# Reordering the loads and splitting one stripe of layer 1 in a fused linear-attention and MLP kernel

## The chip, the cores and the metric

The kernel runs on one core of a Trainium2 chip. The metric is the device time of one execution in microseconds. The kernel before falls into two groups, about 263 us (262.9 to 264.0) and about 265.8 us (265.2 to 266.6). A trace is one execution; its span is about 1.7 us shorter than the time of that execution (263.5 of 265.2 us).

Names used below: TensorE is PE in the profile, its weight loads PEld; VectorE is DVE, ScalarE ACT, GpSimd POOL, and SP issues most transfers. SMELU is the smooth ReLU between the two layers; relu on ScalarE is its first part. A cast turns float32 into bf16.

## The reference

Lightning attention with a decay per head, then a two-layer MLP with a smooth ReLU:

```python
# q, k, v: (4, 8, 768, 64) float32, decay lam: (8,)
# attention, per block: (q kT * decay mask) v + (q * decay) state;  state = decay * state + kT v
x = attn_out.transpose(0, 2, 1, 3).reshape(3072, 512)
h = x @ w_in                      # 512 x 2048
g = where(h >= 1, h, where(h <= -1, 0, (h + 1) ** 2 / 4))
out = g @ w_out                   # 2048 x 512
```

## The kernel before

The 3072 tokens are 24 chunks of 128; four chunks make a stripe of 512 tokens. A chunk has two units `u` (four heads each), and a unit three stages. T transposes q (`pq`), computes kT and the state update in one matmul (`pk`), and copies them out of PSUM. S computes the scores (`ps`) from kT and masks them (`sc`). O computes the output (`po`) and copies it into `xT`, which layer 1 reads. In these traces TensorE ran its instructions in program order, ready or not: in the kernel before, the masked scores of chunk 3's last O were there at 29.5 us, but this O ran at 41.9 us, after chunk 4's `pk` at 41.5 us, which stands before it in the program.

```python
def load(c):                                   # 3 x 256 KB, runs of 256 B, on the SP queue
    for name, src in (("q", q), ("k", k), ("v", v)):
        t = ld.tile([128, H, D], F32, ...)     # 6 buffers each
        nc.sync.dma_start(out=t, in_=...)

def load_w_in(i):  nc.gpsimd.dma_start(...)    # 4 pieces, float32 -> bf16, POOL queue
def load_w_out(i): nc.gpsimd.dma_start(...)    # 4 pieces

def cast(c, k_eng):                            # qs on POOL, ks on DVE or POOL, v on ACT
    ...
    nc.scalar.copy(out=vi[c % NV][:, :, 0, :], in_=vf...)
# ... (cut: stage_t, stage_s, stage_o)
def l1(s, ni):      # four 128x512 matmuls into ph, relu on ACT; smelu: three DVE operations per pair
def l2(s, i):       # four 128x512 matmuls into py
# ...
    ensure_loaded(CPS - 1)                     # CPS = 4 chunks per stripe
    for c in range(CPS):
        ensure_cast(c, nc.vector)
        if c >= 1:
            load_w_in(state["wi"]); state["wi"] += 1
        for _ in range(4): ...                 # attention of chunk c, alone
    load_w_in(state["wi"])
    for i in range(WS): load_w_out(i)
    ensure_loaded(CPS + 1); ensure_cast(CPS)
    a, b_ = att_step()                         # T of chunk 4, then O of chunk 3
    ensure_loaded(CPS + PF)                    # PF = 5
    for s in range(NST + 1):
        for i in range(FO):                    # 16 steps a stripe
            # sub-steps due by now, two a unit: even T(u) and O(u-1), odd S(u); casts one chunk ahead
            if s < NST: l1(s, i)
            for f in todo_a: f()               # T or S
            if s < NST: smelu(s, i)
            if s > 0:   l2(s - 1, i)
            for f in todo_b: f()               # O
```

So in a full stripe each step holds four layer-1 matmuls of stripe s, four layer-2 matmuls of stripe s-1 and half an attention unit.

Of the kernel before, what the change touches and what calls it, by code (L numbers as in the profile page):

```python
# [9 lines left out]
BF16 = mybir.dt.bfloat16  # L10
I32 = mybir.dt.int32
AX = mybir.AluOpType
AF = mybir.ActivationFunctionType


def _bc(ap, idx, n):

    a = list(ap.ap)
    a = a[:idx] + [[0, n]] + a[idx:]
    return bass.AP(ap.tensor, ap.offset, a)  # L20
# [3 lines left out]
def kernel(  # L24
# [16 lines left out]
    nc = tc.nc  # L41
    B, H, S, D = q.shape
    C = 128
# [5 lines left out]
    KO = d_model // 128  # L49
    FO = d_ff // 128  # L50
    MS = 512
    NST = n_tok // MS
    NCH = n_tok // C
    CPS = MS // C
    NU = NCH * 2

    const = ctx.enter_context(tc.tile_pool(name="const", bufs=1))
    big = ctx.enter_context(tc.tile_pool(name="big", bufs=1))
    ld = ctx.enter_context(tc.tile_pool(name="ld", bufs=6))
    qkp = ctx.enter_context(tc.tile_pool(name="qkp", bufs=3))  # L60
    ktp = ctx.enter_context(tc.tile_pool(name="ktp", bufs=3))
    scp = ctx.enter_context(tc.tile_pool(name="scp", bufs=2))
# [14 lines left out]


    qkv_ld = {}

    def load(c):
        b, s0 = c // NCB, (c % NCB) * C
        ts = []
        for name, src in (("q", q), ("k", k), ("v", v)):
            t = ld.tile([128, H, D], F32, name=f"{name}f", tag=f"{name}f")
            nc.sync.dma_start(out=t, in_=src[b, :, s0:s0 + C, :].rearrange("h p d -> p h d"))
            ts.append(t)
        qkv_ld[c] = ts

    lam_b = const.tile([128, H], F32)  # L90
    nc.sync.dma_start(out=lam_b, in_=lam.partition_broadcast(128))
    load(0)
# [44 lines left out]

    def load_w_in(i):
        n = d_ff // WS
        nc.gpsimd.dma_start(out=w_in_sb[:, :, i * n:(i + 1) * n], in_=w_in_r[:, :, i * n:(i + 1) * n])  # L140

    def load_w_out(i):
        n = FO // WS
        nc.gpsimd.dma_start(out=w_out_sb[:, i * n:(i + 1) * n, :], in_=w_out_r[:, i * n:(i + 1) * n, :])


    qs, ks = {}, {}

    def cast(c, k_eng):
        qf, kf, vf = qkv_ld.pop(c)  # L150
        cb = c % NCB
        t = qkp.tile([128, H, D], BF16, name="qs", tag="qs")
        nc.gpsimd.tensor_tensor(t, qf, _bc(tab_q[:, cb, :], 2, D), op=AX.mult)  # L153
        qs[c] = t
        t = qkp.tile([128, H, D], BF16, name="ks", tag="ks")
        k_eng.tensor_tensor(t, kf, _bc(tab_k[:, cb, :], 2, D), op=AX.mult)  # L156
        ks[c] = t
        nc.scalar.copy(out=vi[c % NV][:, :, 0, :], in_=vf.rearrange("p (a b) d -> p a (b d)", b=2))  # L158

# [2 lines left out]
    def stage_t(u):  # L162
        c, hf = u // 2, u % 2
        cb = c % NCB
        pq = pp_q.tile([128, 2, 128], BF16, name="pq", tag="pq")
        pk = pp_k.tile([128, 2, 2, 128], F32, name="pk", tag="pk")
        for j in range(2):
            hp = 2 * hf + j
            nc.tensor.transpose(out=pq[:, j, :], in_=qs[c][:, 2 * hp:2 * hp + 2, :].rearrange("p a d -> p (a d)"),  # L169
                                identity=ident)  # L170
        for j in range(2):
            hp = 2 * hf + j
            nc.tensor.matmul(pk[:, j], lhsT=ks[c][:, 2 * hp:2 * hp + 2, :].rearrange("p a d -> p (a d)"),  # L173
                             rhs=vi[c % NV][:, hp], start=True, stop=True)
        qb = qbd[u % NQ]
        for hi in range(2):
            nc.scalar.copy(out=qb[hi * 64:hi * 64 + 64, :, hi, :], in_=pq[hi * 64:hi * 64 + 64])  # L177
        t = ktp.tile([128, 2, 128], BF16, name="kT", tag="kT")
        nc.scalar.copy(out=t, in_=pk[:, :, 1, :])  # L179
        kT[u] = t  # L180
        if cb < NCB - 1:
            t = up.tile([128, 2, 128], BF16, name="U", tag=f"U{hf}")
            if cb == 0:
                nc.vector.tensor_copy(t, pk[:, :, 0, :])
            else:
                nc.vector.tensor_tensor(t, pk[:, :, 0, :], U[u - 2], op=AX.add)  # L186
            U[u] = t
# [10 lines left out]
    def stage_o(u):  # L198
        c, hf = u // 2, u % 2
        cb = c % NCB  # L200
        st, off = c // CPS, (c % CPS) * C
        po = pp_o.tile([128, 2, 2, 128], F32, name="po", tag="po")
        for j in range(2):
            hp = 2 * hf + j
            if cb > 0:
                nc.tensor.matmul(po[:, j], lhsT=U[u - 2][:, j, :], rhs=qbd[u % NQ][:, j], start=True, stop=False)  # L206
            nc.tensor.matmul(po[:, j], lhsT=vi[c % NV][:, hp, 0, :], rhs=sc_sb[u][:, 2 * j:2 * j + 2, :],  # L207
                             start=(cb == 0), stop=True)
        if st not in xT:
            xT[st] = xp.tile([128, KO, MS], BF16, name="xT", tag="xT")  # L210
        for hi in range(2):
            nc.scalar.copy(out=xT[st][hi * 64:hi * 64 + 64, 2 * hf:2 * hf + 2, off:off + C],  # L212
                           in_=po[hi * 64:hi * 64 + 64, :, hi, :])

    def att(i):

        u, odd = i // 2, i % 2
        a, b_ = [], []
        if not odd:
            if u < NU:  # L220
                a.append(lambda: stage_t(u))
            if 1 <= u <= NU:
                b_.append(lambda: stage_o(u - 1))
        elif u < NU:
            a.append(lambda: stage_s(u))
        return a, b_


    gT, r_t, py_t = {}, {}, {}

    def l1(s, ni):
        ph = pp_h.tile([128, MS], F32, name="ph", tag="ph")
        for ko in range(KO):
            nc.tensor.matmul(ph, lhsT=w_in_sb[:, ko, ni * 128:(ni + 1) * 128], rhs=xT[s][:, ko, :],  # L234
                             start=(ko == 0), stop=(ko == KO - 1))
        if ni % 2 == 0:
            r_t[s] = rp.tile([128, 2, MS], BF16, name="r", tag="r")
        nc.scalar.activation(out=r_t[s][:, ni % 2, :], in_=ph, func=AF.Relu, bias=one[:, 0:1])  # L238

    def smelu(s, ni):  # L240
        if ni % 2 == 0:
            return
        r = r_t[s]
        if ni == 1:
            gT[s] = gp.tile([128, FO, MS], BF16, name="gT", tag="gT")
        t = rp.tile([128, 2, MS], BF16, name="t1", tag="t1")
        nc.vector.tensor_scalar(t, r, 0.5, 1.0, op0=AX.mult, op1=AX.min)
        w = rp.tile([128, 2, MS], BF16, name="w1", tag="w1")
        nc.vector.tensor_tensor(w, r, t, op=AX.subtract)  # L249
        nc.vector.tensor_tensor(gT[s][:, ni - 1:ni + 1, :], w, t, op=AX.mult)  # L250

    def l2(s, i):
        ms, kg = i // 4, i % 4
# [10 lines left out]
            nc.sync.dma_start(out=out[m0:m0 + 128, :], in_=o)  # L264


    PF = 5
    state = {"ld": 2, "cast": 0, "att": 0, "wi": 0, "wo": 0}

    def ensure_loaded(c):  # L270
        while state["ld"] <= min(c, NCH - 1):
            load(state["ld"])
            state["ld"] += 1

    def ensure_cast(c, k_eng=None):
        while state["cast"] <= min(c, NCH - 1):
            cast(state["cast"], k_eng or nc.gpsimd)
            state["cast"] += 1

    def att_step():  # L280
        a, b_ = att(state["att"])
        state["att"] += 1
        return a, b_

    NSUB = 2 * NU + 1


    ensure_loaded(CPS - 1)
    for c in range(CPS):
        ensure_cast(c, nc.vector)  # L290
        if c >= 1:
            load_w_in(state["wi"])
            state["wi"] += 1
        for _ in range(4):
            a, b_ = att_step()
            for f in a + b_:
                f()
    load_w_in(state["wi"])
    for i in range(WS):
        load_w_out(i)  # L300
    ensure_loaded(CPS + 1)
    ensure_cast(CPS)
    a, b_ = att_step()
    for f in a + b_:
        f()
    ensure_loaded(CPS + PF)

    def target(g):

        base = 4 * CPS + 1  # L310
        if g < 16:
            return base + (18 * (g + 1)) // 16
        return min(NSUB, base + 18 + (g - 15))

    for s in range(NST + 1):
        for i in range(FO):
            g = s * FO + i
            todo_a, todo_b = [], []
            while state["att"] < min(NSUB, target(g)):
                c = state["att"] // 4  # L320
                ensure_loaded(c + PF)
                ensure_cast(c + 1)
                a, b_ = att_step()
                todo_a += a
                todo_b += b_
            if s < NST:
                l1(s, i)
            for f in todo_a:
                f()
            if s < NST:  # L330
                smelu(s, i)
            if s > 0:
                l2(s - 1, i)
            for f in todo_b:
                f()


# [28 lines left out]
```

## Time and profile before

| | before |
|---|---|
| time, median of the comparison | 263.62 us (263.03 to 265.84) |
| span of the trace | 263.5 us (an execution of 265.2 us, near the slower group) |
| TensorE busy | 85% |
| first layer-1 matmul | 43.2 us |
| second, third, fourth, fifth stripe begin (first layer-1 matmul that runs beside layer 2, and each 16 steps on) | 78.0, 113.3, 148.6, 183.7 us |
| last layer-1 stripe begins | 217.9 us |

The page's slices cut the span into 40 parts of 6.6 us; a digit is the busy share in tenths. PEclk is the granted TensorE clock; before the first clock record of a trace (22.7 us here) the page counts it as full, which is no measurement.

```profile
PE   0567306666889999999999999999999999999993
...
ACT  4768303778996977797779777977796754554210
...
PEclk9999755999999999999999999999999999999998
DMA  6999999999990526753574357110111011111122
```

From the thirteenth slice on TensorE is full up to the end of the kernel. But for that end, all its idle time is in the first 78 us, in which the DMA engines are full (90% or more in the slices from 6.6 to 79 us). The waits of TensorE in that part, longest first (columns: who waited for whom, total us, times, longest us):

```profile
PE pk L173 <- ACT vi_152 L158: 12.6, 1, 12.6
PE pq L169 <- POOL qs L153: 6.7, 1, 6.7
PE ps L192 <- ACT kT L179: 5.0, 8, 1.9
```

The 12.6 us are chunk 4's v, which landed at 40.9 us behind the weights. Chunk 3's O stands behind chunk 4's T in TensorE's order, so layer 1 could not start either.

In the steady part nothing waits. This is one unit of attention there, on TensorE alone (start, duration, operation):

```profile
116.11 0.28 PE L169 MATMUL pq<-ident,qs 128*128 128x128 bf16 x2
116.22 0.38 PE L173 MATMUL pk<-vi_152,ks 128*128 128x256 bf16 x2
116.44 1.03 PE L258 MATMUL py<-w_out_sb,gT 128*128 128x512 bf16 x4
117.31 0.38 PE L207 MATMUL po<-sc,vi_150 128*128 128x256 bf16 x2
117.53 1.03 PE L234 MATMUL ph<-xT,w_in_sb 128*128 128x512 bf16 x4
118.39 0.38 PE L192 MATMUL ps<-qbd_148,kT 128*128 128x256 bf16 x2
```

The durations overlap: the four `py` matmuls from 116.44 us are listed with 1.03 us, and `po` starts 0.87 us after them. The pace is the difference of starts. Between the transposes (`pq`) and the scores (`ps`) of the unit lie 2.28 us, filled with a layer-2 group, an older O and a layer-1 group. In that time ScalarE copies q (0.74 us) and kT (0.37 us).

### The profile page before, as it was taken

The numbers are of one execution on the slowest core, as the hardware profiler recorded it, in microseconds if no ns is written. First come the engines' busy times: TensorE is split into PE (matmuls) and PEld (weight loads), VectorE is DVE, ScalarE is ACT, GpSimd is POOL, SyncE is SP. The second block draws the span as 40 slices with busy tenths as digits, with TensorE's granted clock in tenths as the row PEclk, the third lists the DMA queues.
The fourth block names the chain that finished last, engine by engine and source line by source line (L and its number), as shares of the span: only waits on it lengthen the run. The fifth ranks groups of instructions, "written<-read, shape, count | busy, mean of one in ns | idle before, by whom it ended". The sixth has DMA issues, their size and how long they took to land.

```text
span 263.5 us, 3576 instructions
## 1 busy us (share of the span) xinstructions
PE 222.8 (85%) x1209; PEld 118.7 (45%) x1232; DVE 143.8 (55%) x245; ACT 173.7 (66%) x389; POOL 54.2 (21%) x61
## 2 busy tenths in 40 slices
PE   0567306666889999999999999999999999999993
PEld 0234203333445555555555555555555544444441
DVE  3554201388887576657574766574747645555300
ACT  4768303778996977797779777977796754554210
POOL 3418111552340332033303320333000000000000
PEclk9999755999999999999999999999999999999998
DMA  6999999999990526753574357110111011111122
GB/s 134 210 217 187 196 196 220 210 226 218 218 202 2 138 67 120 159 128 85 108 159 121 88 113 163 40 40 0 42 41 40 2 40 40 40 42 40 40 80 80
DMA packets 82721, 29.58 MB, mean 112 GB/s; under 512 B 75536, under 2 KB 79632, under 8 KB 82704
## 3 DMA queue, kind: packets, MB, share of 16 engines
q1 hardware_dynamic: 78480, 25.18, 45.5%
q0 software_dynamic: 4224, 4.19, 9.7%
q8 instruction: 9, 0.15, 0.3%
q14 instruction: 8, 0.07, 0.1%
HBM read 27.27 MB, written 6.29 MB: 127 GB/s over the span
## 4 chain that ended last, share of the span: by engine, by line
PE 69%; DVE 3%; ACT 1%; issue 0%; ACTq 0%
PE py L258 31%; PE ph L234 26%; PE po L207 3%; PE ps L192 3%; PE pk L173 2%; PE po L206 2%; PE pq L169 1%; DVE gT L250 1%; DVE w_726 L249 1%; DVE sc L195 0%; DVE w_768 L249 0%; ACT r L238 0%; DVE U L186 0%; ACT xT L212 0%; ACT osb L262 0%
## 5 line engine op out<-in xcount | busy, mean ns | idle before, releaser
L234 PE MATMUL ph<-xT,w_in_sb 128*128 128x512 bf16 x380 | 99.6, 383 | 1.7 <-ACT r L238 1.3
L238 ACT ACTIVATE r<-ph,one 128x512 bf16<-128x512 f32 x96 | 65.9, 687 | 43.3 <-PE ph L234 39.6
L258 PE MATMUL py<-w_out_sb,gT 128*128 128x512 bf16 x365 | 92.3, 379 | 1.0
L234 PEld LDWEIGHTS <-w_in_sb 128*128 128x128 bf16 x384 | 37.9, 99 | 37.6 <-issue 2.8
L258 PEld LDWEIGHTS <-gT 128*128 128x128 bf16 x384 | 37.6, 98 | 32.3
L153 POOL TENSOR_TENSOR qs<-qf,tab_q 128x512 bf16<-128x512 f32 x24 | 25.3, 1052 | 121.7 <-PE pq L169 92.0
L186 DVE TENSOR_TENSOR U<-pk,U 128x256 bf16<-128x256 f32 x32 | 13.6, 424 | 56.5 <-ACT kT L179 56.5
L212 ACT CAST xT<-po 64x256 bf16<-64x256 f32 x96 | 35.3, 367 | 4.5 <-PE po L207 3.7
L195 DVE TENSOR_TENSOR sc<-ps,causal 128x512 bf16<-128x512 f32 x48 | 32.9, 685 | 4.6 <-PE ps L192 4.0
L156 POOL TENSOR_TENSOR ks<-kf,tab_k 128x512 bf16<-128x512 f32 x20 | 22.3, 1117 | 7.9 <-DMA kf<-in_k_dram 7.9
L262 ACT COPY osb<-py 128x512 f32<-128x512 f32 x24 | 14.2, 591 | 12.4 <-PE py L258 12.4
L169 PE MATMUL pq<-ident,qs 128*128 128x128 bf16 x96 | 14.3, 235 | 6.7 <-POOL qs L153 6.7
L179 ACT CAST kT<-pk 128x256 bf16<-128x256 f32 x48 | 17.9, 372 | 2.4 <-PE pk L173 1.3
L173 PE MATMUL pk<-vi_152,ks 128*128 128x256 bf16 x32 | 6.8, 298 | 14.6 <-ACT vi_152 L158 12.6
L169 PEld LDWEIGHTS <-qs 128*128 128x128 bf16 x96 | 10.1, 106 | 16.8 <-POOL qs L153 6.7
L173 PEld LDWEIGHTS <-ks 128*128 128x128 bf16 x96 | 8.1, 103 | 20.5 <-issue 8.1
L192 PEld LDWEIGHTS <-kT 128*128 128x128 bf16 x96 | 8.5, 101 | 19.4 <-ACT kT L179 11.0
L158 ACT CAST vi_152<-vf 128x512 bf16<-128x512 f32 x8 | 4.9, 610 | 11.9 <-DMA vf<-in_v_dram 11.9
L177 ACT COPY qbd_146<-pq 64x256 bf16<-64x256 bf16 x32 | 11.6, 361 | 1.6 <-PE pq L169 1.2
L177 ACT COPY qbd_144<-pq 64x256 bf16<-64x256 bf16 x32 | 11.5, 361 | 0.6 <-PE pq L169 0.2
L177 ACT COPY qbd_148<-pq 64x256 bf16<-64x256 bf16 x32 | 11.5, 361 | 0.5
L206 PEld LDWEIGHTS <-U 128*128 128x128 bf16 x80 | 8.2, 102 | 7.8 <-issue 3.7
(187 smaller groups left out, 213.9 us busy)
## 6 DMA issues: line engine op xcount, KB each, us to landing
qf<-in_q_dram SPq DMA_DIRECT2D x24, 256.0 KB, 4.8
kf<-in_k_dram SPq DMA_DIRECT2D x24, 256.0 KB, 4.7
vf<-in_v_dram SPq DMA_DIRECT2D x24, 256.0 KB, 5.0
out_dram<-osb SPq DMA_DIRECT2D x24, 256.0 KB, 2.0
w_in_sb<-in_moe_w_in_dram POOLq DMA_DIRECT2D x4, 512.0 KB, 8.7
w_out_sb<-in_moe_w_out_dram POOLq DMA_DIRECT2D x4, 512.0 KB, 15.5
lam_b<-in_lam_dram SPq DMA_DIRECT2D x1, 4.0 KB, 2.9
```

Source lines behind the costliest of these rows:

```text
L153: nc.gpsimd.tensor_tensor(t, qf, _bc(tab_q[:, cb, :], 2, D), op=AX.mult)
L156: k_eng.tensor_tensor(t, kf, _bc(tab_k[:, cb, :], 2, D), op=AX.mult)
L169: nc.tensor.transpose(out=pq[:, j, :], in_=qs[c][:, 2 * hp:2 * hp + 2, :].rearrange("p a d -> p (a d)"), identity=ident)
L173: nc.tensor.matmul(pk[:, j], lhsT=ks[c][:, 2 * hp:2 * hp + 2, :].rearrange("p a d -> p (a d)"), rhs=vi[c % NV][:, hp], start=True, stop=True)
L177: nc.scalar.copy(out=qb[hi * 64:hi * 64 + 64, :, hi, :], in_=pq[hi * 64:hi * 64 + 64])
L179: nc.scalar.copy(out=t, in_=pk[:, :, 1, :])
L192: nc.tensor.matmul(ps[:, 2 * j:2 * j + 2, :], lhsT=kT[u][:, j, :], rhs=qbd[u % NQ][:, j], start=True, stop=True)
L195: nc.vector.tensor_tensor(t, ps, _bc(causal, 1, 4), op=AX.mult)
L212: nc.scalar.copy(out=xT[st][hi * 64:hi * 64 + 64, 2 * hf:2 * hf + 2, off:off + C], in_=po[hi * 64:hi * 64 + 64, :, hi, :])
L234: nc.tensor.matmul(ph, lhsT=w_in_sb[:, ko, ni * 128:(ni + 1) * 128], rhs=xT[s][:, ko, :], start=(ko == 0), stop=(ko == KO - 1))
L238: nc.scalar.activation(out=r_t[s][:, ni % 2, :], in_=ph, func=AF.Relu, bias=one[:, 0:1])
L258: nc.tensor.matmul(py, lhsT=gT[s][:, ko, ms * 128:(ms + 1) * 128], rhs=w_out_sb[:, ko, :], start=(ko == 0), stop=(ko == FO - 1))
```

## The change

The intent is to load in the order of need: four token chunks, w_in, four chunks, w_out, the rest. Two loads of SP wait for a weight piece of the POOL queue. While w_out is not there, layer 1 runs alone, and for that stripe 1 is split into halves of 256 tokens, so that its first half needs only chunks 4 and 5. The core of the diff:

```diff
+            if after is not None:
+                tc.add_manual_dep(d.ins, after.ins.name, SYNC)
...
+    nc.scalar.preload_act_table_set("natural_log_exp_and_others")
...
+    items = []                      # t, s, o of every unit, in TensorE's order
+    for u in range(NU):
+        if u % 2 == 0 and u > 0:
+            items += [("o", u - 1), ("t", u)]
+        else:
+            items += [("t", u)] + ([("o", u - 1)] if u > 0 else [])
+        items.append(("s", u))
...
+    def att_to(n):
+        while st["it"] < min(n, len(items)):
+            kind, u = items[st["it"]]
+            if kind == "t" and u % 2 == 0:
+                cast_to(u // 2)                           # casts on demand
+            fns[kind](u)
+            if kind == "s" and u % 2 == 1 and st["ahead"]:
+                cast_to(u // 2 + 1)                       # a chunk ahead, later on
...
+        if c == 1:
+            load_w_in(0); load_w_in(1)
+        elif c == 2:
+            load_w_in(2); load_w_in(3)
+            load_to(CPS, after=w_dma[2])
+            load_to(2 * CPS - 1)
+
+    run(zip_(full(0)[:10], []), 0)                        # layer 1 alone
+    run(zip_(full(0)[10:], []), done(CPS) - st["it"])     # with chunk 4
+    att_to(done(CPS + 1))                                 # chunk 5 alone
+    run(zip_(half(1, 0), []), done(2 * CPS - 1) - st["it"])   # with chunks 6, 7
+    for i in range(WS):
+        load_w_out(i)
+    load_to(2 * CPS, after=w_dma[WS + 2])
+    load_to(2 * CPS + LD - 1)
+    st["ahead"] = True
+    run(zip_(half(1, 1), []), 0)                          # alone
+    run(zip_([], l2s(0)), done(3 * CPS - 1) - st["it"])   # layer 2 with chunks 8 to 11
+    for s in range(2, NST + 1):
+        a = done(min((s + 2) * CPS, NCH) - 1)
+        run(zip_(full(s) if s < NST else [], l2s(s - 1)), a - st["it"])
```

(`run` spreads the attention items over the half-steps; cuts are marked with dots.)

More of the change, by code (lines that the diff above doesn't have):

```diff
@@ L55 @@
     NU = NCH * 2
+    LD = 6
     const = ctx.enter_context(tc.tile_pool(name="const", bufs=1))
     big = ctx.enter_context(tc.tile_pool(name="big", bufs=1))
-    ld = ctx.enter_context(tc.tile_pool(name="ld", bufs=6))
+    ld = ctx.enter_context(tc.tile_pool(name="ld", bufs=LD))
     qkp = ctx.enter_context(tc.tile_pool(name="qkp", bufs=3))
@@ L79, with load @@
     qkv_ld = {}
-    def load(c):
+    w_dma = []
+    SYNC = mybir.DependencyInfo(mybir.DependencyClass.Sync, mybir.DependencyReason.DATA)
+    def load(c, after=None):
         b, s0 = c // NCB, (c % NCB) * C
@@ L85, in load @@
             t = ld.tile([128, H, D], F32, name=f"{name}f", tag=f"{name}f")
-            nc.sync.dma_start(out=t, in_=src[b, :, s0:s0 + C, :].rearrange("h p d -> p h d"))
+            d = nc.sync.dma_start(out=t, in_=src[b, :, s0:s0 + C, :].rearrange("h p d -> p h d"))
+            if after is not None:
+                tc.add_manual_dep(d.ins, after.ins.name, SYNC)
+                after = None
             ts.append(t)
         qkv_ld[c] = ts
+    nc.scalar.preload_act_table_set("natural_log_exp_and_others")
     lam_b = const.tile([128, H], F32)
@@ L139, in load_w_in, with cast @@
         n = d_ff // WS
-        nc.gpsimd.dma_start(out=w_in_sb[:, :, i * n:(i + 1) * n], in_=w_in_r[:, :, i * n:(i + 1) * n])
+        w_dma.append(nc.gpsimd.dma_start(out=w_in_sb[:, :, i * n:(i + 1) * n],
+                                         in_=w_in_r[:, :, i * n:(i + 1) * n]))
     def load_w_out(i):
         n = FO // WS
-        nc.gpsimd.dma_start(out=w_out_sb[:, i * n:(i + 1) * n, :], in_=w_out_r[:, i * n:(i + 1) * n, :])
+        w_dma.append(nc.gpsimd.dma_start(out=w_out_sb[:, i * n:(i + 1) * n, :],
+                                         in_=w_out_r[:, i * n:(i + 1) * n, :]))
     qs, ks = {}, {}
-    def cast(c, k_eng):
+    def cast(c):
         qf, kf, vf = qkv_ld.pop(c)
@@ L155, in cast @@
         t = qkp.tile([128, H, D], BF16, name="ks", tag="ks")
-        k_eng.tensor_tensor(t, kf, _bc(tab_k[:, cb, :], 2, D), op=AX.mult)
+        (nc.vector if c < CPS else nc.gpsimd).tensor_tensor(t, kf, _bc(tab_k[:, cb, :], 2, D), op=AX.mult)
         ks[c] = t
@@ L200, in stage_o @@
         cb = c % NCB
-        st, off = c // CPS, (c % CPS) * C
+        sx, off = c // CPS, (c % CPS) * C
         po = pp_o.tile([128, 2, 2, 128], F32, name="po", tag="po")
@@ L208, in stage_o, with l1, smelu @@
                              start=(cb == 0), stop=True)
-        if st not in xT:
-            xT[st] = xp.tile([128, KO, MS], BF16, name="xT", tag="xT")
+        if sx not in xT:
+            xT[sx] = xp.tile([128, KO, MS], BF16, name="xT", tag="xT")
         for hi in range(2):
-            nc.scalar.copy(out=xT[st][hi * 64:hi * 64 + 64, 2 * hf:2 * hf + 2, off:off + C],
+            nc.scalar.copy(out=xT[sx][hi * 64:hi * 64 + 64, 2 * hf:2 * hf + 2, off:off + C],
                            in_=po[hi * 64:hi * 64 + 64, :, hi, :])
-    def att(i):
-        u, odd = i // 2, i % 2
-        a, b_ = [], []
-        if not odd:
-            if u < NU:
-                a.append(lambda: stage_t(u))
-            if 1 <= u <= NU:
-                b_.append(lambda: stage_o(u - 1))
-        elif u < NU:
-            a.append(lambda: stage_s(u))
-        return a, b_
     gT, r_t, py_t = {}, {}, {}
-    def l1(s, ni):
+    def l1(s, ni, hf):
         ph = pp_h.tile([128, MS], F32, name="ph", tag="ph")
-        for ko in range(KO):
-            nc.tensor.matmul(ph, lhsT=w_in_sb[:, ko, ni * 128:(ni + 1) * 128], rhs=xT[s][:, ko, :],
-                             start=(ko == 0), stop=(ko == KO - 1))
-        if ni % 2 == 0:
+        n, sl = (1, slice(0, MS)) if hf is None else (2, slice(hf * MS // 2, (hf + 1) * MS // 2))
+        for j in range(n):
+            for ko in range(KO):
+                nc.tensor.matmul(ph[:, j * MS // n:(j + 1) * MS // n],
+                                 lhsT=w_in_sb[:, ko, (ni + j) * 128:(ni + j + 1) * 128],
+                                 rhs=xT[s][:, ko, sl], start=(ko == 0), stop=(ko == KO - 1))
+        i = (ni // n) % 2
+        if i == 0:
             r_t[s] = rp.tile([128, 2, MS], BF16, name="r", tag="r")
-        nc.scalar.activation(out=r_t[s][:, ni % 2, :], in_=ph, func=AF.Relu, bias=one[:, 0:1])
-    def smelu(s, ni):
-        if ni % 2 == 0:
+        nc.scalar.activation(out=r_t[s][:, i, :], in_=ph, func=AF.Relu, bias=one[:, 0:1])
+    def smelu(s, ni, hf):
+        n, sl = (1, slice(0, MS)) if hf is None else (2, slice(hf * MS // 2, (hf + 1) * MS // 2))
+        if (ni // n) % 2 == 0:
             return
         r = r_t[s]
-        if ni == 1:
+        if s not in gT:
             gT[s] = gp.tile([128, FO, MS], BF16, name="gT", tag="gT")
@@ L249, in smelu @@
         nc.vector.tensor_tensor(w, r, t, op=AX.subtract)
-        nc.vector.tensor_tensor(gT[s][:, ni - 1:ni + 1, :], w, t, op=AX.mult)
+        v4 = (lambda x: x) if hf is None else (lambda x: x.rearrange("p a (b m) -> p (a b) m", b=2))
+        nc.vector.tensor_tensor(gT[s][:, ni - n:ni + n, sl], v4(w), v4(t), op=AX.mult)
     def l2(s, i):
@@ L264, in l2 @@
             nc.sync.dma_start(out=out[m0:m0 + 128, :], in_=o)
-    PF = 5
-    state = {"ld": 2, "cast": 0, "att": 0, "wi": 0, "wo": 0}
-    def ensure_loaded(c):
-        while state["ld"] <= min(c, NCH - 1):
-            load(state["ld"])
-            state["ld"] += 1
-    def ensure_cast(c, k_eng=None):
-        while state["cast"] <= min(c, NCH - 1):
-            cast(state["cast"], k_eng or nc.gpsimd)
-            state["cast"] += 1
-    def att_step():
-        a, b_ = att(state["att"])
-        state["att"] += 1
-        return a, b_
@@ L285 @@
-    NSUB = 2 * NU + 1
-    ensure_loaded(CPS - 1)
-    for c in range(CPS):
-        ensure_cast(c, nc.vector)
-        if c >= 1:
-            load_w_in(state["wi"])
-            state["wi"] += 1
-        for _ in range(4):
-            a, b_ = att_step()
-            for f in a + b_:
-                f()
-    load_w_in(state["wi"])
+    items = []
[5 more added lines that the diff above has]
+        items.append(("s", u))
@@ new lines @@
+    items.append(("o", NU - 1))
+    pos_of = {it: i for i, it in enumerate(items)}
+    fns = {"t": stage_t, "s": stage_s, "o": stage_o}
+    st = {"it": 0, "cast": 0, "ld": 2, "ahead": False}
+    def att_to(n):
[6 more added lines that the diff above has]
+                cast_to(u // 2 + 1)
+            st["it"] += 1
@@ new lines, in cast_to, with load_to, done, run @@
+    def cast_to(c):
+        while st["cast"] <= min(c, NCH - 1):
+            cast(st["cast"])
+            st["cast"] += 1
+            if st["ahead"]:
+                load_to(st["cast"] - 1 + LD)
+    def load_to(c, after=None):
+        while st["ld"] <= min(c, NCH - 1):
+            load(st["ld"], after)
+            st["ld"] += 1
+    def done(c):
+        return pos_of[("o", 2 * c + 1)] + 1
+    def run(steps, n_att):
+        a0, ns = st["it"], len(steps)
+        for i, (f1, f2) in enumerate(steps):
+            if f1 is not None:
+                l1(*f1)
+            att_to(a0 + (n_att * (2 * i + 1)) // (2 * ns))
+            if f1 is not None:
+                smelu(*f1)
+            if f2 is not None:
+                l2(*f2)
+            att_to(a0 + (n_att * (2 * i + 2)) // (2 * ns))
@@ new lines, in full, with half, l2s, zip_ @@
+    def full(s):
+        return [(s, ni, None) for ni in range(FO)]
+    def half(s, hf):
+        return [(s, ni, hf) for ni in range(0, FO, 2)]
+    def l2s(s):
+        return [(s, i) for i in range(FO)]
+    def zip_(a, b):
+        n = max(len(a), len(b))
+        return list(zip(a + [None] * (n - len(a)), b + [None] * (n - len(b))))
+    load_to(CPS - 1)
+    for c in range(CPS):
+        att_to(done(c) - (2 if c < CPS - 1 else 0))
+        if c == 1:
+            load_w_in(0)
+            load_w_in(1)
+        elif c == 2:
+            load_w_in(2)
+            load_w_in(3)
+            load_to(CPS, after=w_dma[2])
+            load_to(2 * CPS - 1)
@@ L299 @@
+    run(zip_(full(0)[:10], []), 0)
+    run(zip_(full(0)[10:], []), done(CPS) - st["it"])
+    att_to(done(CPS + 1))
+    run(zip_(half(1, 0), []), done(2 * CPS - 1) - st["it"])
     for i in range(WS):
         load_w_out(i)
-    ensure_loaded(CPS + 1)
-    ensure_cast(CPS)
-    a, b_ = att_step()
-    for f in a + b_:
-        f()
-    ensure_loaded(CPS + PF)
-    def target(g):
-        base = 4 * CPS + 1
-        if g < 16:
-            return base + (18 * (g + 1)) // 16
-        return min(NSUB, base + 18 + (g - 15))
@@ L315 @@
-    for s in range(NST + 1):
-        for i in range(FO):
-            g = s * FO + i
-            todo_a, todo_b = [], []
-            while state["att"] < min(NSUB, target(g)):
-                c = state["att"] // 4
-                ensure_loaded(c + PF)
-                ensure_cast(c + 1)
-                a, b_ = att_step()
-                todo_a += a
-                todo_b += b_
-            if s < NST:
-                l1(s, i)
-            for f in todo_a:
-                f()
-            if s < NST:
-                smelu(s, i)
-            if s > 0:
-                l2(s - 1, i)
-            for f in todo_b:
-                f()
+    load_to(2 * CPS, after=w_dma[WS + 2])
```

## The prediction

> **What bounds it now.** The busy table gives TensorE 85% of 263.5 us. The slices and the chain of waits show two regimes. From 78 us to 259 us TensorE never waits: one stripe (16 layer-1 steps, 16 layer-2 steps, four token chunks) takes 35.5 us, the sum of its matmuls (128x512 issues every 0.216 us; attention about 1.9 us a chunk). Before 78 us only about 30 us of TensorE work is done, so about 48 us are idle: the start (first matmul 6.7 us), 12.6 us in one piece (28.9 to 41.5 us, the waits: pk on the vi cast, whose v landed at 40.9 us behind w_in and w_out), and a stretch from 43 to 78 us in which ScalarE is 80 to 96% busy. All the gain has to come from those 48 us.
>
> **What the change does.**
> 1. Chunks 0-3, w_in, chunks 4-7, w_out. The 12.6 us hole goes: attention of chunk 3 no longer sits behind chunk 4's loads. But all four w_in pieces are now queued by about 15 us, beside chunks 2 and 3. The queue table gives about 97 ns a weight packet and 24 ns a token packet; [...]: behind w_out a 256 KB token load took 6.5 to 9 us instead of 1.14. So chunk 3's v, landing at 24.2 us now, should land at 28 to 31 us; layer 1 starts at 34 to 38 us instead of 43.2 us. Gain 5 to 9 us.
> 2. Layer 1 of stripe 0 starts alone (10 steps, about 10 us), then chunk 4 in 6 steps (about 10 us), chunk 5 alone (about 6.5), half of stripe 1 with chunks 6-7 (about 15, ScalarE and VectorE bound: relu 0.69, 4.4 us of ScalarE a chunk, SMELU groups 1.8 to 2.8 us), the other half alone (about 7.5).
> 3. Layer 2 of stripe 0 then runs without layer 1, with chunks 8-11. Scores follow their transposes directly; from transpose to kT is about 1.5 us (qbd 0.76, kT 0.37, latency), which nothing hides. I estimate 6.6 us a chunk against 5.4 us of matmuls: 26 us. Before, this layer was packed with layer 1 without a hole.
> 4. In the steady stripes scores of even units come one 0.86 us group after their transposes instead of about three: about 0.3 us of stall, four times a stripe.
> 5. One table load (1.28 us) less, off the critical path: the first v lands at 7.3 us.
> The halves' 256-wide matmuls cost about the same TensorE time.
>
> **Sum (estimate from these durations).** Layer 2 of stripe 0 ends at about 36 + 78 = 114 us, as now (113.5 us), with half a chunk less attention done (+1.4 us) and 3 to 4 us of new stalls later. The earlier start is given back.
>
> Predicted 268 us, 257 to 277. Faster by over 2%: 0.15; within 2%: 0.42; slower by over 2%: 0.43.
>
> **What would show it.** Step 1: no wait over 5 us of pk on vi; first layer-1 matmul at 34 to 38 us; chunk 3's v landing near 30 us. Steps 2-3: between that and 114 us TensorE 60 to 70% busy, the layer-2-only stretch 24 to 29 us long, ps waiting on kT with 1 us or more each. Step 4: stripes of 36 to 38 us instead of 35.5, ps waiting on kT after 120 us, where none is now.
>
> **What would make it wrong.** Faster: tokens keep a larger share against w_in (layer 1 at 31 us), or the prelude overlaps better than I laid out. Slower: in-order ScalarE falls behind in the steady stripes, or chunks 8-11 wait for w_out.

114 us against 113.5 is +0.5, so 263.6 + 0.5 + 1.4 + 3.5 gives about 269, written as 268. Two statements are to be read with the traces. From 43 to 78 us in the kernel before ScalarE was busy for 27.7 of 35.0 us (79%), in windows of 5 us between 25 and 98%. And eight 256-wide matmuls of the changed kernel took 0.88 us up to the next start (71.30 to 72.18 us), four 512-wide ones 0.87 us in the kernel before (116.44 to 117.31 us).

## The result

The changed kernel takes 280.14 us (279.12 to 280.27, four runs) against 263.62 us. The ratio is 1.060, 95% interval 1.053 to 1.067: 6% slower. Ratios in this document are the mean time of one kernel's fast runs over that of the other's in the same rounds, so they are not quite the ratio of the quoted medians. The spans of the two traces differ by 14.8 us (278.3 and 263.5), less than the medians, because the trace of before is of a 265.2 us execution.

The slices after (7.0 us each), the same rows:

```profile
PE   0566698767687888889999999999999999999994
...
ACT  2566557774775667778777777787777775444311
...
PEclk9999999975979999999999999999999999999999
DMA  7999990099999466662465332010001001000111
```

The hole of before is gone, and after the first slice none before 120 us is as empty as it was. But TensorE is full only from about 120 us on. The granted clock falls to half twice, from 59.8 to 70.0 us and from 76.8 to 80.2 us, and the DMA engines all but stand still for two slices at 42 to 56 us (11 and 4 GB/s). The stretches of the new schedule, read with the windows view (columns: window, its length, then busy us and instruction count of PE, PEld, DVE, ACT and POOL, the granted clock, DMA share, GB/s):

```profile
35.10:46.90 11.80, 11.79 (x43) 4.65 (x43) 7.43 (x12) 7.43 (x12) 2.90 (x3) 1.00 0.79 130
46.90:56.70 9.80, 6.72 (x40) 3.70 (x40) 8.06 (x14) 7.13 (x15) 5.72 (x6) 1.00 0.11 12
56.70:63.40 6.70, 4.12 (x22) 2.14 (x20) 3.20 (x5) 4.42 (x12) 0.19 (x1) 0.73 1.19 189
63.40:84.70 21.30, 15.31 (x102) 11.40 (x100) 12.48 (x18) 13.29 (x30) 6.85 (x6) 0.77 1.20 217
84.70:92.80 8.10, 7.49 (x66) 6.23 (x65) 5.83 (x11) 5.43 (x9) 0.00 (x0) 1.00 1.05 166
92.80:120.00 27.20, 22.48 (x144) 13.08 (x146) 10.65 (x19) 19.06 (x48) 8.17 (x8) 1.00 0.61 146
```

In order these are layer 1 alone, layer 1 with chunk 4, chunk 5 alone, the half stripe with chunks 6 and 7, the other half alone, and layer 2 alone with chunks 8 to 11. The clock of 1.00 in the first row is not measured before 39.3 us: there is no record, and the layer-1 steps ran at half pace (1.71 us a step, 0.87 us later). The fourth row is the worst: 21.3 us, and no engine is above 72% busy. Its first half on TensorE:

```profile
65.72 0.42 PE L178 MATMUL pq<-ident,qs 128*128 128x128 bf16 x2
67.26 0.58 PE L182 MATMUL pk<-vi_151,ks 128*128 128x256 bf16 x2 [1.12 <-ACT vi_151 L167]
67.64 1.91 PE L233 MATMUL ph<-xT,w_in_sb 128*128 128x256 bf16 x8
69.34 0.63 PE L201 MATMUL ps<-qbd_145,kT 128*128 128x256 bf16 x2
...
71.30 1.04 PE L233 MATMUL ph<-xT,w_in_sb 128*128 128x256 bf16 x8
72.18 0.38 PE L201 MATMUL ps<-qbd_147,kT 128*128 128x256 bf16 x2
74.32 0.39 PE L216 MATMUL po<-sc,vi_151 128*128 128x256 bf16 x2 [1.76 <-DVE sc L204]
```

The bracket gives the idle time before an instruction and what ended it. Three things are in these lines. `pk` waits for the cast of v. Eight 256-wide matmuls take 1.91 us where the same eight take 1.04 us a little later: that is the half clock (granted 0.50 from 67.6 to 69.3 us, 1.00 from 71.3 to 72.2 us). And O waits for the masked scores, which stand behind a SMELU group on VectorE.

In layer 2 alone the scores follow their transposes directly, and the wait is in the open (the first unit of chunk 9):

```profile
100.45 0.28 PE L178 MATMUL pq<-ident,qs 128*128 128x128 bf16 x2
100.56 0.38 PE L182 MATMUL pk<-vi_151,ks 128*128 128x256 bf16 x2
102.14 0.39 PE L201 MATMUL ps<-qbd_145,kT 128*128 128x256 bf16 x2 [1.19 <-ACT kT L188]
```

In the steady stripes one layer-1 group lies between transposes and scores, and the stripe's first layer-1 group itself waits for xT, whose last O has only just been issued:

```profile
157.52 0.59 PE L233 MATMUL ph<-xT,w_in_sb 128*128 128x512 bf16 x2
158.57 0.59 PE L233 MATMUL ph<-xT,w_in_sb 128*128 128x512 bf16 x2 [0.46 <-ACT xT L221]
...
159.86 0.28 PE L178 MATMUL pq<-ident,qs 128*128 128x128 bf16 x2
159.97 0.38 PE L182 MATMUL pk<-vi_153,ks 128*128 128x256 bf16 x2
160.19 1.03 PE L233 MATMUL ph<-xT,w_in_sb 128*128 128x512 bf16 x4
161.38 0.39 PE L201 MATMUL ps<-qbd_149,kT 128*128 128x256 bf16 x2 [0.16 <-ACT kT L188]
```

From `pq` to `ps` are 1.52 us here against 2.28 before; the layer-1 group was through at 161.05 us (0.86 us after its start), so TensorE stood for 0.33 us.

The account of the 14.8 us of span, with the starts of the stripes (before: 113.31, then 217.85 us; after: 119.96, then 232.10 us):

| | before | after | difference |
|---|---|---|---|
| until the third stripe begins | 113.3 | 120.0 | +6.7 |
| the three stripes with attention | 104.5 | 112.1 | +7.6 |
| last layer-1 stripe to the end | 45.7 | 46.2 | +0.5 |

Of the 7.6 us about 1.3 are not a loss of pace: at that point the kernel before is ahead by T of two units and S and O of one, two thirds of a chunk (an estimate, at 1.9 us of TensorE a chunk).

### The profile page after: what moved, and what is told of

Read it like the earlier page. It is cut to its first block, busy times and chain, and to the rows that moved or that the text cites. A ratio compares the mean times of both kernels' runs of the same rounds, so it can differ in the third digit from the quotient of the medians.

```text
span 278.3 us, 3689 instructions
## 1 busy us (share of the span) xinstructions
PE 235.5 (85%) x1275; PEld 125.6 (45%) x1296; DVE 148.8 (53%) x245; ACT 177.5 (64%) x388; POOL 63.0 (23%) x61
## 3 DMA queue, kind: packets, MB, share of 16 engines
q1 hardware_dynamic: 78480, 25.18, 42.1%
q0 software_dynamic: 4224, 4.19, 9.3%
## 5 line engine op out<-in xcount | busy, mean ns | idle before, releaser
L233 PE MATMUL ph<-xT,w_in_sb 128*128 128x512 bf16 (+1 forms) x443 | 101.9, 361 | 3.5 <-ACT xT L221 3.1
L162 POOL TENSOR_TENSOR qs<-qf,tab_q 128x512 bf16<-128x512 f32 x24 | 30.5, 1272 | 138.7 <-PE pq L178 94.2
L233 PEld LDWEIGHTS <-w_in_sb 128*128 128x128 bf16 x448 | 45.6, 102 | 35.8 <-issue 8.7
L261 PEld LDWEIGHTS <-gT 128*128 128x128 bf16 x384 | 37.6, 98 | 36.8
L165 POOL TENSOR_TENSOR ks<-kf,tab_k 128x512 bf16<-128x512 f32 x20 | 25.7, 1286 | 0.6 <-PE ps L201 0.2
L265 ACT COPY osb<-py 128x512 f32<-128x512 f32 x24 | 14.1, 585 | 12.7 <-PE py L261 12.6
L178 PE MATMUL pq<-ident,qs 128*128 128x128 bf16 x96 | 14.8, 242 | 6.8 <-POOL qs L162 6.8
L201 PEld LDWEIGHTS <-kT 128*128 128x128 bf16 x96 | 7.4, 102 | 24.6 <-ACT kT L188 21.0
L216 PE MATMUL po<-sc,vi_153 128*128 128x256 bf16 x32 | 8.4, 287 | 3.5 <-DVE sc L204 3.3
L193 DVE CAST U<-pk 128x256 bf16<-128x256 f32 x8 | 3.4, 420 | 14.8 <-ACT kT L188 14.8
```

The source lines that it names most:

```text
L162: nc.gpsimd.tensor_tensor(t, qf, _bc(tab_q[:, cb, :], 2, D), op=AX.mult)
L165: (nc.vector if c < CPS else nc.gpsimd).tensor_tensor(t, kf, _bc(tab_k[:, cb, :], 2, D), op=AX.mult)
L178: nc.tensor.transpose(out=pq[:, j, :], in_=qs[c][:, 2 * hp:2 * hp + 2, :].rearrange("p a d -> p (a d)"), identity=ident)
L233: nc.tensor.matmul(ph[:, j * MS // n:(j + 1) * MS // n], lhsT=w_in_sb[:, ko, (ni + j) * 128:(ni + j + 1) * 128], rhs=xT[s][:, ko, sl], sta ...
L261: nc.tensor.matmul(py, lhsT=gT[s][:, ko, ms * 128:(ms + 1) * 128], rhs=w_out_sb[:, ko, :], start=(ko == 0), stop=(ko == FO - 1))
L265: nc.scalar.copy(out=o, in_=py)
```

## The experiments

The first theory (A) was mine: the loads are innocent and the compute order costs the time, because work that ran side by side now runs one after the other, and waits that were covered are open. The rival (B) was the load order itself: w_in beside chunks 2 and 3, an idle load queue, a late w_out. All kernels gave correct results.

| run | what | us, median | ratio to before, 95% interval |
|---|---|---|---|
| changed kernel | | 280.14 | 1.060 (1.053 to 1.067) |
| e1_loads_only | loads of the change, compute order of before | 260.98 | 0.989 (0.981 to 0.996) |
| e2_schedule_only | compute order of the change, loads of before | 280.56 | 1.063 (1.055 to 1.071) |
| e3_old_spacing | change, old spacing from stripe 2 | 275.35 | 1.043 (1.035 to 1.050) |
| e4_repacked | change, stripe 1 packed again | 275.36 | 1.042 (1.032 to 1.052) |
| e5_idle_matmuls | change, extra matmuls in idle time | 279.08 | 1.058 (1.050 to 1.065) |
| e8_cast_ahead | change, casts a chunk ahead | 275.20 | 1.044 (1.038 to 1.049) |
| e10_spacing_and_cast | e3 and e8 | 273.46 | 1.039 (1.036 to 1.042) |
| e11_all_packed | e10, stripe 1 packed again | 269.61 | 1.025 (1.020 to 1.030) |
| e6_one_wait | e1, chunks 8 and 9 before w_out | 256.12 | 0.971 (0.966 to 0.977) |
| e7_strict_order | e6, w_in after chunk 3; 8 steps alone | 263.96 | 1.003 (0.996 to 1.010) |
| e9_strict_hold4 | e7, 4 steps alone | 258.89 | 0.982 (0.979 to 0.986) |
| e12_strict_early4 | e9, chunk 4 after the second w_in piece | 257.98 | 0.980 (0.978 to 0.982) |

### Loads or compute order: e1 and e2

e1 against the kernel before:

```diff
-        if c >= 1:
-            load_w_in(state["wi"]); state["wi"] += 1
+        if c == 1:
+            load_w_in(0); load_w_in(1)
+        elif c == 2:
+            load_w_in(2); load_w_in(3)
+            load(CPS, after=w_dma[2]); state["ld"] += 1
+            ensure_loaded(2 * CPS - 1)
...
+                if state["wo"] == 0 and state["cast"] == 2 * CPS:   # once, in the main loop
+                    state["wo"] = 1
+                    for j in range(WS): load_w_out(j)
+                    load(2 * CPS, after=w_dma[WS + 2])
```

> The kernel before with the change's load order only (four chunks, w_in, four chunks, w_out, cross-queue waits); compute order as before. Theory A (the loads are innocent or good, the new compute order costs the time): layer 1 starts at 34 to 36 us as in the changed kernel, the steady stripes begin 8 to 14 us earlier than before's 78 us, time 249 to 257 us. Rival B (the load order itself costs: w_in beside chunks 2 and 3, a load queue that stands idle, w_out and chunk 8 late): 264 us or more.

e2 against the changed kernel:

```diff
-        if c == 1: ... elif c == 2: ...        # w_in two by two, chunk 4 waits
+        if c >= 1:
+            load_w_in(c - 1)
+    load_w_in(WS - 1)
+    for i in range(WS): load_w_out(i)
+    load_to(2 * CPS + 1)
-    load_to(2 * CPS, after=w_dma[WS + 2])      # later: no second wait either
```

> The changed kernel's compute order with the loads of before (w_in and w_out queued together by 23 us, no cross-queue waits). Theory A: chunk 3's v lands at 24 us again, so layer 1 starts at about 31 us instead of 35; everything after it as in the changed kernel: 274 to 279 us. Rival B: with the old loads most of the loss goes, 262 to 269 us.

The two kernels settle the first question. With the old loads the new compute order still takes 280.56 us, and with the new loads the old compute order takes 260.98 us. The whole loss comes from the compute order; B falls. But both sizes missed. In e2 layer 1 started at 33.7 us, not 31. In e1 layer 1 started at 35.9 us, 7 us earlier than before, and most of that was lost again, as these waits of e1 between 34 and 75 us show (TensorE first, ScalarE second):

```profile
PE ps L199 <- ACT kT L186: 9.2, 6, 6.2
```

```profile
ACT vi L165 <- DMA vf<-in_v_dram: 5.3, 1, 5.3
```

Chunk 8's v now lands at 62.2 us, behind w_out, because of the second cross-queue wait. ScalarE, in order, stands with its cast until 62.2 us, and the kT of a unit whose `pk` ran at 56.9 us stands behind that cast. The hole of 12.6 us became a hole of about 6 us at another chunk.

### The spacing in the stripes: e3

```diff
-    for s in range(2, NST + 1):
-        a = done(min((s + 2) * CPS, NCH) - 1)
-        run(zip_(full(s) if s < NST else [], l2s(s - 1)), a - st["it"])
+    for s in range(2, NST + 1):
+        for i in range(FO):          # as before: one sub-step a step, T and O(u-1), then S(u)
+            goal = 48 + (18 * (g + 1) // 16 if g < 16 else 18 + g - 15)
+            ...
```

> The changed kernel, but from the third stripe on the attention pieces are spread as before (one sub-step a step, running two sub-steps ahead of the stripe). Theory A: the three stripes with attention take 35.3 to 36.5 us instead of 37.1 to 37.6, no wait of scores on kT or of layer 1 on xT there; 273 to 276 us, that is 4.5 to 7 us less than the change. Rival (all of the loss is made before 120 us and the small waits in the stripes are covered by slack): 279 to 281 us.

275.35 us, inside the expectation, 4.8 us less than the change. The trace is more careful than the time. The three stripes took 39.3, 35.7 and 35.0 us instead of 37.6, 37.1 and 37.5: the second and third lost their waits, but the first, which runs 18 sub-steps in 16 steps, got a wait of 1.5 us for kT and one of 1.0 us for a v cast where two sub-steps fall into one step. Together with the last stripe, that starts without a wait, this is 2.8 us. Another 2.3 us came before the third stripe (117.7 instead of 120.0 us), where the edit changes nothing; there the clock of this execution fell once (61.1 to 71.4 us) and not a second time, as in the trace of the change. So the spacing is shown to cost some 2.8 us net in this trace; that the rest of the 4.8 is due to it is not shown.

### The casts: e8

```diff
-            if kind == "s" and u % 2 == 1 and st["ahead"]:
-                cast_to(u // 2 + 1)
+            if kind == "s" and u % 2 == 1 and u // 2 >= CPS:
+                cast_to(min(u // 2 + 1, NCH - 1 if st["ahead"] else 2 * CPS - 1))
```

> The changed kernel with the casts of chunks 5, 6 and 7 put a chunk ahead, as the kernel before does all along and the change only from chunk 8 on. Theory D (the rest of what I mis-sized: each chunk's kT|U matmul waits 1.1 to 1.4 us for its v cast, which stands behind the last chunk's output copies on ScalarE): those waits of chunks 5 to 7 go and the time falls by 2.5 to 4.5 us, to 275.5 to 277.5 us. Rival (the wait is covered by the next one in the chain): 279 to 281 us.

275.20 us, 4.9 us less than the change, a little more than expected. The half stripe with chunks 6 and 7 fell from 21.3 to 16.2 us. Its window in e8, same columns as above, and the same unit of chunk 6 on TensorE:

```profile
62.90:79.10 16.20, 11.64 (x103) 9.25 (x101) 12.17 (x19) 12.69 (x29) 6.14 (x6) 1.00 1.14 216
```

```profile
64.53 0.28 PE L178 MATMUL pq<-ident,qs 128*128 128x128 bf16 x2
64.64 0.38 PE L182 MATMUL pk<-vi,ks 128*128 128x256 bf16 x2
64.86 1.04 PE L233 MATMUL ph<-xT,w_in_sb 128*128 128x256 bf16 x8
66.56 0.39 PE L201 MATMUL ps<-qbd,kT 128*128 128x256 bf16 x2 [0.66 <-ACT kT L188]
```

From transposes to scores it now takes 2.03 us; in the changed kernel it took 3.62. The wait for the cast is gone, and the clock stayed up in this stretch although nothing was done about it (it fell for 3.4 us just after it). The data of these casts had landed long before (in the changed kernel v of chunks 5 to 7 landed at 35.9, 39.9 and 43.6 us, and `pk` waited for their casts until 58.4, 67.3 and 76.9 us): the cast only stood, in ScalarE's order, behind the relu and the output copies of the chunk before. What e8 does not remove is O's wait for the masked scores: 3.3 us of this stretch in the changed kernel, 2.7 us in e8. SMELU operations that run longer beside GpSimd casts are part of what stands before them: in the traces of before and of the change the 128x1024 operations with two inputs took 0.69 us wherever no GpSimd instruction overlapped them, and up to 1.42 us where one did (at 74.6 us in the changed kernel, beside a cast of 1.30 us), and the operation with one input at 70.6 us, which stands before the scores of the 1.76 us wait, took 1.26 us instead of 0.42. No run tests that alone.

### The clock: e5

```diff
+    def warm(n):                     # pp_y is not in use yet
+        for _ in range(n):
+            nc.tensor.matmul(warm_ps[0], lhsT=ident, rhs=xT[0][:, 0, :], start=True, stop=True)
...
+            if 2 * (CPS + 1) <= u < 4 * CPS and kind in ("t", "s"):
+                warm(2)
```

> The changed kernel with two extra 128x512 matmuls, into a PSUM bank not yet in use, after each transpose and score group of chunks 5 to 7: useless work in the time in which TensorE waits, so that its clock stays up. Theory C (part of what I mis-sized is that the sparse stretch from 56 to 85 us runs at a granted clock of 0.67): the clock there goes to 0.9 or more, the half stripe with chunks 6 and 7 takes 16 to 18.5 us instead of 21.3, time 275 to 278 us. Rival (the chain over ScalarE and VectorE alone sets the pace; the clock is a by-product): 279.5 us or more.

The clock came up, to 1.00 in the half stripe (0.77 in the changed kernel), which then took 19.0 us:

```profile
62.60:81.60 19.00, 14.67 (x116) 11.02 (x117) 11.84 (x18) 13.42 (x30) 7.59 (x6) 1.00 1.17 212
```

But the times scatter from 276.9 to 280.7 us, median 279.08, between the two expectations. This is inconclusive for the total. In the trace, which is of the fastest of the four executions (276.94 us), about 2.3 of the 5.1 us that e8 took out of this stretch go with the clock alone, with the extra matmuls counted against it; `pk` still waits 2.4 us for the casts, and the other 2.8 us came only with e8. (The 0.67 of the expectation is the clock from 60 to 80 us; from 56 to 85 us it is 0.76.)

### Packing: e4, e10 and e11

e4 against the changed kernel:

```diff
-    att_to(done(CPS + 1))
-    run(zip_(half(1, 0), []), done(2 * CPS - 1) - st["it"])
+    att_to(done(2 * CPS - 1))                       # chunks 5, 6, 7 alone
...
-    run(zip_(half(1, 1), []), 0)
-    run(zip_([], l2s(0)), done(3 * CPS - 1) - st["it"])
+    run(zip_(full(1), l2s(0)), done(3 * CPS - 1) - st["it"])
```

> The changed kernel, but layer 1 of stripe 1 is whole and runs step by step with layer 2 of stripe 0 and chunks 8 to 11; chunks 5, 6, 7 run alone before. Theory A: the third stripe begins at 109 to 113 us instead of 120, time 269 to 273 us. Rival (the packing of the two layers is not where time was lost): within 2 us of the change, 278 to 282 us.

275.36 us: 4.8 us less than the change, where 7 to 11 were expected. The third stripe begins at 116.5 us instead of 120.0. Chunks 5 to 7 alone took 21.7 us, 7.2 us a chunk, at a granted clock of 0.59; the prediction had about 6.5 us for chunk 5 alone.

e10 is e3 and e8 together:

> The changed kernel with both repairs at once: the old spacing of the attention from the third stripe on, and the casts of chunks 5 to 7 a chunk ahead. If the two losses are separate, they add: 4.8 + 4.9 us off 280.1, 269 to 272 us, near what I had predicted for the change (268). If they are one loss seen twice: 274 us or more.

273.46 us (272.18 to 274.41): between the two expectations. The two repairs do not add up fully: 6.7 us, not 9.7. The first of the three stripes again took 39.3 us for the reason given under e3, and the part before the third stripe is like that of e8 (it begins at 114.9 us; in e8 at 115.7).

e11 is e10 with the edit of e4 in the old spacing:

> The run before it with layer 1 of stripe 1 packed with layer 2 of stripe 0 again, in the old spacing. Theory A (the rest of the loss is work that no longer runs beside other work): a further 4 to 8 us, 262 to 267 us, about the kernel before. Rival (packing is worth nothing once the spacing and the casts are right): 269 us or more.

269.61 us: 3.9 us less than e10, just short of the 4 to 8 expected, and above the range that I gave: the time lies in the rival's range of 269 us or more. That packing is worth nothing is still not what was seen, as the four times of e11 (269.1 to 272.0 us) and of e10 (272.2 to 274.4 us) don't overlap. Most of what is left above the kernel before is in the early part: in the trace the third stripe begins at 116.6 us, 3.2 us late, and the three stripes after that add 1.2 us. Chunks 5 to 7 still run alone, from 55 to 73 us, and the granted clock from 57 to 77 us is 0.68. That this remainder is due to them is argued from the trace and was not tested by itself.

### A better kernel: e6, e7, e9, e12

e6 is e1 without the second cross-queue wait, so that chunks 8 and 9 are loaded straight after chunk 7 and fill the idle load queues:

```diff
                     for j in range(WS): load_w_out(j)
-                    load(2 * CPS, after=w_dma[WS + 2])
-                    state["ld"] += 1
```

(and the cap on `ensure_loaded`, which held chunks 8 and 9 back, is removed)

> The loads-only kernel without the second cross-queue wait: chunks 8 and 9 are loaded before w_out and fill the time in which the load queues stood idle. If the loads-only kernel gained only 2 us because its hole was moved to chunk 8 (landing at about 63 us behind w_out): the hole goes, the stripes begin at 64 to 67 us instead of 74, time 249 to 254 us. If w_out then comes too late for layer 2 instead: 257 us or more.

256.12 us, 2.9% faster than the kernel before and the fastest of all. It missed its range by 2 us: the third stripe begins at 104.1 us, against 113.3 before and 109.3 in e1. The slices show TensorE full from the twelfth slice (of 6.4 us) on and no gap in the loads until w_out is in:

```profile
PE   0566477588799999999999999999999999999993
...
DMA  6999999999999367347625734011011101111112
```

e7 also holds w_in back until chunk 3's k has landed, and runs eight layer-1 steps alone. It loads only chunks 4 and 5 early, where e6 loads 4 to 7, and spreads the attention of the first two stripes anew, so that its distance to e6 has more than one cause:

```diff
+            tc.add_manual_dep(w_dma[0].ins, ld_dma[("k", CPS - 1)].ins.name, SYNC)
...
+    HOLD = 8                          # layer-1 steps before the attention of chunk 4
```

> As the run before it, but w_in is held back until chunk 3's k has landed [...], eight layer-1 steps run alone, then chunks 4 to 7 with the other eight. If the share of w_in is what delays layer 1: first layer-1 matmul at 27 to 30 us instead of 36, stripes begin at 58 to 62 us, time 243 to 250 us. If ScalarE and the chain of the attention set the pace from there: no gain over the run before it, 250 us or more.

Layer 1 started at 28.2 us, as expected, 7 us earlier than in e6, and the kernel was 7.8 us slower than e6, in the range of the second alternative. The eight steps were through by 40 us, and then chunks 4 to 7 took 32 us with only eight steps left to fill their waits:

```profile
40.00:71.90 31.90, 18.81 (x103) 10.56 (x106) 17.49 (x29) 20.94 (x51) 13.47 (x14) 0.79 1.20 204
```

In that window TensorE waited 13.4 us for kT, in eight waits of up to 3.1 us. This looks like the changed kernel's fault made by hand: an early start is spent on the filler (independent work that could cover waits), and the chain behind it lies bare. e9 tests it: it leaves twelve steps for the filling, and e12 also lets chunk 4 load one w_in piece earlier:

```diff
-    HOLD = 8
+    HOLD = 4                          # e9 and e12
-            load(CPS, after=w_dma[2])
+            load(CPS, after=w_dma[1])     # e12 only
```

> The strict-order kernel with four layer-1 steps alone instead of eight, so that twelve are left to run beside the attention of chunks 4 to 7. If the strict order lost its 8 us because attention and layer 1 ran one after the other (31 us for chunks 4 to 7 with eight steps): stripes begin at 63 to 68 us instead of 72, time 251 to 257 us. If it is the arrival of chunks 4 to 8 that sets the time: no change, 261 us or more.

> As the run before it, but chunk 4's loads wait for the second w_in piece instead of the third. If the wait for chunk 4 after the four steps matters: 1 to 3 us faster than the run before it; if its loads only take turns with w_in: within 1 us of it.

e9 took 258.89 us: 5.1 us less than e7, for four steps moved; a little above its range but not at the other alternative's 261, and the stripes begin at 68.5 us, just outside the 63 to 68. e12 took 257.98 us, 0.9 us less, which is within the 1 us of the rival. Starting layer 1 seven microseconds earlier gained nothing in these two kernels: e6, which starts it at 35.1 us and spreads it, is still ahead.

## Why the prediction was right or wrong

The direction was right, but hardly more than by luck: slower by over 2% had 0.43 and within 2% 0.42, and the 268 us itself is only 1.7% slower. The size was not right: a range of 257 to 277 us was given, and 280.14 was measured.

- **What bounds the kernel**: right. The gain could only come from the first 78 us, and the kernels with the better order took it there.
- **Step 1, the loads**: right. Chunk 3's v landed at 28.7 us (28 to 31 predicted), layer 1 started at 35.1 us (34 to 38), the wait of 12.6 us went. The queue table of the kernel before gives 97 ns a weight packet and 24 ns a token packet (9.7% and 45.5% of 16 engines' 263.5 us, over 4224 and 78480 packets). That weights get most of the time while both are queued was the author's estimate, and the trace of the change shows it: from 16 to 25 us, with both queued, the engines moved 1403 weight packets and 1404 token packets, and the weights had 75% of the packet time, as a weight packet took 94.0 ns there and a token packet 30.6 ns. In the kernel before, k and v of chunk 4, 256 KB each, took 9.2 and 6.6 us beside the weights, from one landing to the next (25.1, 34.2, 40.8 us); from 49 to 76 us, with no weights queued, a token load took 1.2 us on average. And e7, where w_in waits, moved the start to 28.2 us.
- **Step 2, layer 1 alone and in halves**: this is the step that failed. Term by term:

| term of the sum | predicted | measured |
|---|---|---|
| layer 1 alone until chunk 4's transposes | about 10 | 11.8 |
| chunk 4 in 6 steps | about 10 | 9.8 |
| chunk 5 alone | about 6.5 | 6.7 |
| "half of stripe 1 with chunks 6-7" | about 15 | 21.3 |
| the other half | about 7.5 | 8.1 |
| layer 2 alone with chunks 8-11 | 26 | 27.1 |

  The terms add up to 75; I had allowed 78 and got 84.8. The mis-sized term is the half stripe. I had called it bound by ScalarE and VectorE and counted their work. It was bound by a chain: the cast of v, kT, the scores, each behind other work on its engine, with `pk` waiting 1.1 to 1.2 us for the cast in each of the two chunks, O 1.5 to 1.8 us for the masked scores, and half the clock for about half of the stretch. e8 puts the casts ahead and gets 16.2 us, close to the 15. The clock is part of it: it was granted at half from 59.8 to 70.0 us and from 76.8 to 80.2 us, and in the 3.4 us before these falls TensorE was busy for 36 and 40%, with no wait above 1.8 us from 56 to 92 us. What makes it fall was not tested. At its early start, where no clock is recorded, layer 1 ran at half pace: from 35.1 us with 1.71 us a step, about 4 us later with 0.87 us, which is also most of the 1.8 us in the first row. How much of the half stripe is the clock by itself stays open; e5 gives 2.3 us in the trace and nothing certain in time.
- **Step 3, layer 2 without layer 1**: right. 27.1 us against 26, with waits of 1.19 us for kT.
- **Step 4, steady stripes**: the mechanism was right, the size too small. The stripes took 37.6, 37.1 and 37.5 us, inside the 36 to 38 that I gave, but I then put 3 to 4 us into the sum where 6.3 were measured (7.6 less the 1.3 of attention). The missing term is the wait of the first layer-1 group of a stripe for xT, 2.1 us in four stripes, 1.7 of it in these three: the new order finishes a stripe's last O immediately before the layer 1 that reads it; the old one ran two sub-steps ahead.
- **The table load**: the trace of before has two (at 0.81 and 3.96 us, 1.28 us each), that of the change one. The first v landed at 7.33 and 7.36 us: no effect was seen, as predicted; it was not tested alone.
- **The sum**: the prediction's own terms give 263.6 + 0.5 + 1.4 + 3.5, about 269, and I wrote 268. The distance to 280.1 is then 11 us: 6.2 from the part before the third stripe (in which 84.8 us of stretches stand against the 78 allowed, 6.3 of the excess in the half stripe), 2.7 from the later waits, 0.5 from the end, and 1.6 from comparing a trace of before at 265.2 us with a median of 263.6.
- **The check "TensorE 60 to 70% busy"** failed: the windows from 35 to 120 us add up to 67.9 of 84.9 us, 80%. The busy figure counts each matmul to its end in the profile: in the kernel before a 128x512 one is listed with 0.38 us, though the next one started 0.216 us after it, and with 0.63 us at half the clock (44 to 46 us). So in the half stripe TensorE is 72% busy, though its 64 layer-1 matmuls at 0.108 us and two chunks of attention at 1.9 us are about 10.7 of 21.3 us.

## What to carry to other kernels

Filler is a resource: layer-1 groups that run alone at an early start are missing later, where a chain of copies on ScalarE and VectorE has to be covered (13.4 us of waits for kT in e7), so an earlier start counted here only where the work behind it stayed interleaved (e6 256.12 us, e7 263.96 us). When work is moved, read for every dependent pair how much independent work lies between its ends, before and after, and put casts and copies whose data is already there ahead of the work that waits (4.9 us in e8). Moving a load to a later place moved its hole with it (e1, 260.98 us) until something filled the queue in the meantime (e6, 256.12 us).
